# Softmax weights scaled on ScalarE ahead of the transposes, in place of a reciprocal that is spread, transposed and multiplied in after the values

## The chip, the cores and the metric

The kernel runs on one core of one Trainium2 chip. The metric is the device time of one execution in microseconds (us), lower is better; a kernel's time is the median of its runs. The engines of the core are named as the profile names them: PE (TensorE, with its weight loads as PEld), DVE (VectorE), ACT (ScalarE), POOL (GpSimd) and SP (SyncE, which only issues DMAs here). Each has its own in-order queue.

## What is computed

Attention over 4 batches and 8 heads with 576 rows of 64 numbers, in which every row keeps its 32 largest scores; then a feed-forward part over 2304 tokens; then a part with eight experts, of which each token uses at most one. Cut to the lines of the attention, which the change is in, and of the part that runs beside it:

```python
scores = scale * np.matmul(q, k.transpose(0, 1, 3, 2))
kth = np.partition(scores, -top_k, axis=-1)[..., -top_k:-top_k + 1]
mask = scores >= kth
scores = np.where(mask, scores, -1000000000.0)
scores = scores - np.max(scores, axis=-1, keepdims=True)
attn = np.exp(scores)
attn = attn / (np.sum(attn, axis=-1, keepdims=True) + 1e-09)
return np.matmul(attn, v).astype(np.float32)
...
h = x @ w_in
g = np.maximum(h, 0.0) + alpha * np.minimum(h, 0.0)
return (g @ w_out).astype(np.float32)
```

The division by the sum can be done before the product with v or after it; the change moves it from after to before.

## The kernel before

**Units.** The attention is cut into 80 units (class `Unit`). A full unit is 128 rows of q of two heads (one pair) of a batch; a mixed unit (`mix`, 16 of the 80) holds the last 64 rows of both heads as one 128-row block, so it has one "head" of 576 columns where a full unit has two. The 80 units lie in eight work items, two for each batch: blocks 0 and 1 of the rows for the four pairs (8 full units), then blocks 2, 3 and the mixed one (12 units).

**What one unit does, by its methods.** `scores` (PE) makes q times k in PSUM; `copy` (ACT) brings it to SBUF as `sb`; `fold` and `round` (DVE) find the 32nd largest of each row; `exp` (ACT) writes the exponentials to `Ex`; `weights` (DVE) zeroes what lies under the threshold and adds up each row's sum into `st`; `recip` (DVE) takes the reciprocals; `spread` (ACT) writes them as a block `rb` 128 columns wide; `turn` (PE) transposes `Ex` in eight or four pieces plus a last one, and behind that `rb` (L523) or, in a mixed unit, the reciprocals themselves (L526); `evac` (ACT) copies the transposes from PSUM to `PT`, and the transposed reciprocals to `R` (L538, L543); `values` (PE) multiplies with v into `px`; `out` multiplies `px` by `R` on DVE into `xf` (L560), ACT rounds that to `xh` (the tile `x`, L562), and POOL later subtracts the two for the low half (L111).

**What sets the order.** `main` walks over steps; in step kx it works on units kx-2 to kx+2 at once. A step has 14 slots. The table `STEP` says at which slot which method runs, and for which unit: `(5, -1, "turn", 0)` is slot 5 of the step, for the unit one behind. After each slot's methods `slot` puts in pieces of the feed-forward part from the queue `todo`, against a budget: six matmuls at a time, first of the up projection (`up`, L628, with a Relu on ACT, L638, the second half of the activation on DVE, L641, a rounding to `g` on ACT, L647, and a subtraction on POOL, L111), then of the down projection (`down`, L674, copied out by ACT, L683). The up projection writes to two PSUM banks (`pm`), and a bank is free again when L641 has read it. So each engine's order is fixed when the program is built, and at run time an engine waits only where what it needs isn't there yet. While the first work item's units run, `todo` also holds the conversion of the feed-forward weights (L281 to L304).

The routing (`rows`), and after the attention the experts, follow; neither is touched.

## Time and profile before

| | |
|---|---|
| median of 3 runs | 1017.21 us (1016.46 to 1017.65) |
| the profiled execution | 1015.15 us, of which the profile's span is 1013.4 us |
| busy in the span | PE 889.1 us (88%), DVE 825.0 (81%), ACT 624.8 (62%), POOL 347.1 (34%) |
| mean granted TensorE clock | 0.957 of full speed |

By time: up to some 150 us the weights are converted beside the first units; from there to some 820 us attention units and feed-forward run together; then the feed-forward of the last work item and the experts remain. Busy time is the time in which an engine had an instruction under way. Instructions overlap with the next one's start, so what an instruction takes of its engine is read from start to start, and is shorter than its own duration. The chain that ended last is followed back from the end of the program: at each step to what released it, or to the instruction before it on its engine.

### The profile page before, as it was taken

The page shows a single profiled execution, that of the slowest core. Times are in us where ns is not written, and L with a number is a line of the kernel's source. Part 1 is how long each engine was busy: PE and PEld are TensorE (multiplying, and loading weights), DVE is VectorE, ACT ScalarE, POOL GpSimd, SP SyncE. Part 2 cuts the span into 40 slices and gives each one's busy share as a digit, 9 for nine tenths or more (in the row PEclk, how much of TensorE's full clock was granted, in tenths as well). Part 3 has the DMA queues.
Part 4 walks back from the last instruction along what each step waited for, and adds up shares of the span by engine and source line. Part 5 has one row for each costly group of instructions (what it writes and reads, how often), then busy time and mean ns, then how long its engine had stood idle before and what let it go on. Part 6 is the DMA issues. An engine that isn't in the chain of part 4 may idle for free.

```text
span 1013.4 us, 21379 instructions
## 1 busy us (share of the span) xinstructions
PE 889.1 (88%) x7074; PEld 786.7 (78%) x7074; DVE 825.0 (81%) x2859; ACT 624.8 (62%) x1669; POOL 347.1 (34%) x544
## 2 busy tenths in 40 slices
PE   4335569899999989999998899999978999999995
PEld 2234458798999889989997899899978988987541
DVE  5999999999998899989997999899799632366410
ACT  7869767666775567667655766775566434365320
POOL 4866653322430243234212432431133134023100
PEclk9976679999999899999999999999999999999998
DMA  8978985666656476766655676765564769979994
GB/s 244 329 261 239 309 261 188 219 227 185 245 190 236 143 228 204 243 219 214 220 198 159 219 227 234 241 224 192 181 189 179 250 230 416 352 243 384 398 398 149
DMA packets 133321, 244.90 MB, mean 242 GB/s; under 512 B 58831, under 2 KB 91599, under 8 KB 116817
## 3 DMA queue, kind: packets, MB, share of 16 engines
q1 hardware_dynamic: 129824, 239.42, 69.7%
q0 software_dynamic: 2176, 3.73, 1.0%
q8 instruction: 58, 0.95, 0.4%
q14 instruction: 63, 0.51, 0.2%
q10 hardware_dynamic: 1200, 0.30, 0.1%
HBM read 215.00 MB, written 28.92 MB: 241 GB/s over the span
## 4 chain that ended last, share of the span: by engine, by line
PE 59%; DVE 25%; ACT 4%; DMA 2%; issue 2%; POOL 1%; SPq 0%; POOLq 0%; DVEq 0%; ACTq 0%
PE pm L674 20%; PE pm L628 10%; DVE v L461 6%; PE px L553 5%; PE pm L1018 5%; PE ps L1018 4%; DVE Ex L494 4%; PE ps L431 3%; PE pt L520 3%; DVE ra L641 3%; DVE F L464 3%; DVE F L452 3%; DVE m L452 2%; PE ps L425 1%; PE px L549 1%
## 5 line engine op out<-in xcount | busy, mean ns | idle before, releaser
L628 PE MATMUL pm<-x,wr 128*128 128x256 f32 (+1 forms) x1536 | 248.5, 309 | 24.4 <-DVE ra L641 18.5
L628 PEld LDWEIGHTS pm<-x,wr 128*128 128x128 f32 x1536 | 214.9, 193 | 36.4 <-DVE ra L641 23.8
L674 PE MATMUL pm<-g,wr 128*128 128x256 f32 (+1 forms) x1536 | 234.5, 302 | 1.8 <-DVE ra L641 1.2
L674 PEld LDWEIGHTS pm<-g,wr 128*128 128x128 f32 x1536 | 208.9, 189 | 7.0 <-issue 4.6
L461 DVE MAX8 v<-F 128x8 f32<-128x72 f32 (+2 forms) x576 | 213.1, 405 | 0.9
L111 POOL TENSOR_TENSOR g<-ra,g 128x256 fp32r<-128x256 f32 (+1 forms) x128 | 103.2, 815 | 198.7 <-DVE st L499 59.8
L464 DVE MATCH_REPLACE8 F<-v,F 128x72 f32<-128x72 f32 (+1 forms) x432 | 122.9, 290 | 0.0
L494 DVE SCALAR_TENSOR_TENSOR Ex<-sb,v,Ex 128x577 f32<-128x577 f32 x144 | 122.2, 876 | 0.0
L436 ACT ACTIVATE sb<-ps 128x288 f32<-128x288 f32 x224 | 80.0, 411 | 67.9 <-PE ps L431 53.8
L486 ACT ACTIVATE Ex<-sb,st 128x576 f32<-128x576 f32 x144 | 104.8, 775 | 0.1
L647 ACT ACTIVATE g<-ra 128x256 fp32r<-128x256 f32 (+1 forms) x128 | 57.3, 448 | 72.6 <-DVE ra L641 70.4
L532 ACT ACTIVATE PT<-pt 128x512 f32<-128x512 f32 x144 | 86.7, 603 | 22.4 <-PE pt L520 22.0
L111 POOL TENSOR_TENSOR x<-xf,x 128x128 fp32r<-128x128 f32 (+1 forms) x80 | 37.3, 467 | 176.4 <-DVE st L499 120.7
L641 DVE SCALAR_TENSOR_TENSOR ra<-ra,slope,pm 128x256 f32<-128x256 f32 (+1 forms) x128 | 64.7, 507 | 38.7 <-ACT ra L638 38.1
L553 PE MATMUL px<-PT,vt 128*64 128x128 f32 (+1 forms) x1280 | 90.2, 288 | 0.0
L520 PE MATMUL pt<-ident,Ex 128*128 128x128 f32 x576 | 85.1, 281 | 4.3 <-ACT sb L436 4.3
L431 PE MATMUL ps<-kT,qT 64*128 64x288 f32 x576 | 80.0, 349 | 7.0 <-ACT kT L341 2.5
L553 PEld LDWEIGHTS px<-PT,vt 128*64 128x64 f32 x1280 | 70.8, 149 | 9.8 <-issue 2.0
L431 PEld LDWEIGHTS ps<-kT,qT 64*128 64x128 f32 x576 | 61.8, 212 | 20.8 <-issue 9.4
L638 ACT ACTIVATE ra<-pm 128x256 f32<-128x256 f32 (+1 forms) x128 | 52.6, 411 | 38.8 <-PE pm L628 37.4
L520 PEld LDWEIGHTS pt<-ident,Ex 128*128 128x128 f32 x576 | 70.3, 146 | 6.4 <-ACT sb L436 5.9
L452 DVE TENSOR_TENSOR F<-m 128x144 f32<-128x144 f32 (+2 forms) x240 | 66.0, 327 | 0.0
(356 smaller groups left out, 1484.4 us busy)
## 6 DMA issues: line engine op xcount, KB each, us to landing
wr<-win SPq DMA_DIRECT2D x64, 1024.0 KB, 5.1
wr<-wout SPq DMA_DIRECT2D x64, 1024.0 KB, 5.0
wd<-in_moe_w_dram SPq DMA_DIRECT2D x40, 512.0 KB, 11.5
wraw<-in_moe_w_dram SPq DMA_DIRECT2D x32, 512.0 KB, 7.9
wr<-in_moe_w_in_dram SPq DMA_DIRECT2D x16, 512.0 KB, 5.5
vt<-in_v_dram SPq DMA_DIRECT2D x32, 256.0 KB, 2.8
win<-cv SPq DMA_DIRECT2D x16, 512.0 KB, 4.5
wr<-in_moe_w_out_dram SPq DMA_DIRECT2D x16, 512.0 KB, 5.0
```

Of the source, the lines that this page charges most:

```text
L111: i = nc.gpsimd.tensor_tensor(o, a, b, op=OP.subtract)
L431: nc.tensor.matmul(self.ps[h, j][:, 0:HALF], lhsT=hd["q"][gp, a, u * 128 - hd["c0"]:(u + 1) * 128 - hd["c0"]], rhs=hd["k"][gp, b_, c0:c0 + ...
L452: gate[0] = nc.vector.tensor_tensor(o[:, n_], a[:, n_, 0:w], a[:, n_, w:2 * w], op=op)
L461: nc.vector.max(v8[:, h, r, :], F[:, h, 0:w])
L464: nc.vector.match_replace(out=F[:, h, 0:w], in_to_replace=v8[:, h, r, :], in_values=F[:, h, 0:w], imm_value=NEG)
L486: nc.scalar.activation(self.Ex[:, h, :], self.sb[:, h, :], AF.Exp, bias=self.st[:, 0, h:h + 1], scale=0.125)
L494: nc.vector.scalar_tensor_tensor(self.Exp[:, cs], self.sbp[:, cs], v8[:, h, 3, 7:8], self.Exp[:, cs], op0=OP.is_ge, op1=OP.mult, accum_out ...
L520: nc.tensor.transpose(pt[:, c * 128:(c + 1) * 128], P[:, c0:c0 + 128], ident)
L553: nc.tensor.matmul(x[h * 64:(h + 1) * 64, 0:n], lhsT=hd["vt"][:, h, c, :], rhs=rhs, start=False, stop=(c == SF - 1))
L628: nc.tensor.matmul(hp[:, 0:n], lhsT=w[:, (f % 2) * 8 + a * 4 + d, :], rhs=x[:, d, c0:c1], start=(i == 0), stop=(i == 3 * KD - 1))
L641: nc.vector.scalar_tensor_tensor(ra, ra, slope[:, f:f + 1], hp[:, 0:n], op0=OP.mult, op1=OP.add)
L674: nc.tensor.matmul(op_[:, 0:n], lhsT=w[:, 2 * f + a, :], rhs=g[(hf + ch) * 8 + f, sg][:, gg, 0:n], start=(i == 0), stop=(i == ni - 1))
```

## The change

Units from number 8 on (`NORM = 8`; `early`) no longer carry their reciprocals past the product with v. `recip` runs for them at the end of their own step, right behind `weights`, in place of slot 2 of the next step. A new method `norm` at slot 4 of the next step multiplies `Ex` by the reciprocals in place on ACT, one instruction for each head (576 columns; a mixed unit has one). `spread`, the transposes of `rb` or `st`, the copies to `R` and the multiplication on DVE are left out for them. `out` then has ACT read `px` twice, once rounding to `x`, once into `xf`. The first 8 units keep the old way. For all units the table moves `turn` from slots 5, 6 and 8 to 7, 8 and 10, and `evac` from slots 7, 8 and 10 to 9, 10 and 12.

```diff
--- before.py
+++ after.py
@@ -22,15 +22,15 @@
 NSLOT = 14
 STEP = [(0, 0, "exp", 0), (0, 0, "exp", 1), (0, 1, "fold"),
         (1, -2, "values"), (1, 2, "scores"), (1, 0, "certify"),
-        (2, -1, "recip"), (2, 1, "round", 0), (2, 2, "copy", 0),
+        (2, -1, "recip", 0), (2, 1, "round", 0), (2, 2, "copy", 0),
         (3, 2, "copy", 1),
-        (3, 0, "heads", 0), (4, 1, "round", 1),
-        (5, -1, "spread"), (5, -1, "turn", 0), (5, 0, "heads", 1),
-        (6, 1, "round", 2), (6, -1, "turn", 1),
-        (7, -1, "evac", 0),
-        (8, -2, "out"), (8, -1, "evac", 1), (8, 1, "round", 3), (8, 1, "rest"), (8, -1, "turn", 2),
-        (10, 0, "weights", 0), (10, -1, "evac", 2),
-        (11, 0, "weights", 1)]
+        (3, 0, "heads", 0), (4, -1, "norm"), (4, 1, "round", 1),
+        (5, -1, "spread"), (5, 0, "heads", 1),
+        (6, 1, "round", 2), (7, -1, "turn", 0),
+        (8, -2, "out"), (8, -1, "turn", 1), (8, 1, "round", 3), (8, 1, "rest"),
+        (9, -1, "evac", 0), (10, -1, "evac", 1), (10, -1, "turn", 2),
+        (10, 0, "weights", 0), (11, 0, "weights", 1), (11, 0, "recip", 1), (12, -1, "evac", 2)]
+NORM = 8
 AHEAD = 4
 EC = 32
 PH = 6
@@ -408,6 +408,7 @@
             self.exact, self.vi, self.lastu, self.end = exact, vi, lastu, False
             self.mix = u == SF
             self.nh = 1 if self.mix else 2
+            self.early = exact or ai >= NORM
             self.n_ = slice(0, self.nh)
             self.pt = {}
 
@@ -494,13 +495,20 @@
                 nc.vector.scalar_tensor_tensor(self.Exp[:, cs], self.sbp[:, cs], v8[:, h, 3, 7:8], self.Exp[:, cs],
                                                op0=OP.is_ge, op1=OP.mult, accum_out=st[:, 1, h:h + 1])
 
-        def recip(self):
+        def recip(self, at):
             st = self.st
-            nc.vector.reciprocal(st[:, 2, self.n_], st[:, 1, self.n_])
+            if at == self.early:
+                nc.vector.reciprocal(st[:, 2, self.n_], st[:, 1, self.n_])
+
+        def norm(self):
+
+            if self.early:
+                for h in range(self.nh):
+                    nc.scalar.activation(self.Ex[:, h, :], self.Ex[:, h, :], AF.Copy, scale=self.st[:, 2, h:h + 1])
 
         def spread(self):
             st = self.st
-            if not self.mix:
+            if not self.mix and not self.early:
                 self.rb = att.tile([128, 2, 64], F32, name="rb", tag="rb", bufs=2)
                 nc.scalar.activation(self.rb, st[:, 2, :, None].to_broadcast([128, 2, 64]), AF.Copy)
 
@@ -520,10 +528,12 @@
                     nc.tensor.transpose(pt[:, c * 128:(c + 1) * 128], P[:, c0:c0 + 128], ident)
             elif not self.mix:
                 nc.tensor.transpose(pt[:, 0:128], P[:, SB:SB + 128], ident)
-                nc.tensor.transpose(pt[:, 128:256], self.rb.rearrange("p h c -> p (h c)"), ident)
+                if not self.early:
+                    nc.tensor.transpose(pt[:, 128:256], self.rb.rearrange("p h c -> p (h c)"), ident)
             else:
                 nc.tensor.transpose(pt[0:64, 0:128], Ex[:, 0, SB:S], ident)
-                nc.tensor.transpose(pt[:, 128:256], self.st[:, 2, 0:1].to_broadcast([128, 128]), ident)
+                if not self.early:
+                    nc.tensor.transpose(pt[:, 128:256], self.st[:, 2, 0:1].to_broadcast([128, 128]), ident)
 
         def evac(self, h):
             PT, pt = self.PT, self.pt.get(h)
@@ -531,16 +541,18 @@
                 if h < self.nh:
                     nc.scalar.activation(PT[:, 4 * h:4 * h + 4, :].rearrange("p a b -> p (a b)"), pt, AF.Copy)
                 return
-            R = att.tile([128, 128], F32, name="R", tag="R", bufs=1)
-            self.R = R
+            if not self.early:
+                self.R = R = att.tile([128, 128], F32, name="R", tag="R", bufs=1)
             if not self.mix:
                 nc.scalar.activation(PT[:, 8, :], pt[:, 0:128], AF.Copy)
-                nc.scalar.activation(R, pt[:, 128:256], AF.Copy)
+                if not self.early:
+                    nc.scalar.activation(R, pt[:, 128:256], AF.Copy)
             else:
                 for g in range(2):
                     gp = slice(g * 64, (g + 1) * 64)
                     nc.scalar.activation(PT[gp, 8, 0:64], pt[0:64, g * 64:(g + 1) * 64], AF.Copy)
-                    nc.scalar.activation(R[gp, 0:64], pt[gp, 128 + g * 64:128 + (g + 1) * 64], AF.Copy)
+                    if not self.early:
+                        nc.scalar.activation(R[gp, 0:64], pt[gp, 128 + g * 64:128 + (g + 1) * 64], AF.Copy)
 
         def values(self):
             hd, PT = self.hd, self.PT
@@ -557,9 +569,13 @@
             n = 64 if self.mix else 128
             cols = slice(self.col, self.col + n)
             xf = att.tile([128, 128], F32, name="xf", tag="xf", bufs=2)
-            nc.vector.tensor_tensor(xf[:, 0:n], self.x[:, 0:n], self.R[:, 0:n], op=OP.mult)
             xh, xl = self.getx()
-            nc.scalar.activation(xh[:, self.p, cols], xf[:, 0:n], AF.Copy)
+            if self.early:
+                nc.scalar.activation(xh[:, self.p, cols], self.x[:, 0:n], AF.Copy)
+                nc.scalar.activation(xf[:, 0:n], self.x[:, 0:n], AF.Copy)
+            else:
+                nc.vector.tensor_tensor(xf[:, 0:n], self.x[:, 0:n], self.R[:, 0:n], op=OP.mult)
+                nc.scalar.activation(xh[:, self.p, cols], xf[:, 0:n], AF.Copy)
 
             def low():
                 sub(xl[:, self.p, cols], xf[:, 0:n], xh[:, self.p, cols].bitcast(F32))
```

How the order changes. Names in the rows: `sb` scores in SBUF, `Ex` exponentials, `st` sums and reciprocals, `pt` and `ps` PSUM tiles, `kT`, `raw` transposed k and its copy for the low half, `pm` a bank of the feed-forward part. Lines of the changed file are up to 16 higher.

**ACT**, in one step of batch 2 in which the up projection runs, from the last copy of the scores on. Before:

```order
L436 ACTIVATE sb_138<-pt 128x288
L647 ACTIVATE g<-ra 128x320
L341 ACTIVATE kT<-ps 128x512
L342 ACTIVATE raw__6611<-ps 128x512
L505 ACTIVATE rb<-st 128x128
L638 ACTIVATE ra<-pm 128x320
L532 ACTIVATE PT<-pt 128x512
L562 ACTIVATE x<-xf 128x128
L532 ACTIVATE PT<-pt 128x512
```

and now:

```order
L437 ACTIVATE sb_138<-pt 128x288
L507 ACTIVATE Ex_144<-Ex_144,st 128x576 x2
L663 ACTIVATE g<-ra 128x320
L341 ACTIVATE kT<-ps 128x512
L342 ACTIVATE raw__6511<-ps 128x512
L654 ACTIVATE ra<-pm 128x320
L574 ACTIVATE x<-px 128x128
L575 ACTIVATE xf<-px 128x128
L470 ACTIVATE st<-v_6424 128x2
L663 ACTIVATE g<-ra 128x320
L542 ACTIVATE PT<-pt 128x512
```

The two scalings stand right behind the copies of the scores and ahead of the next Relu (L638, now L654); `rb` is gone, `out` is two copies from `px`, and the copies to `PT` come later.

**PE**, the same step, from the transposes of k to the product with v. Before:

```order
L356 MATMUL ps<-ident,nat 128x128 x4
L628 MATMUL pm<-x,wr 128x320 x6
L520 MATMUL pt<-ident,Ex_144 128x128 x8
L628 MATMUL pm<-x,wr 128x320 x6
L522 MATMUL ps<-ident,Ex_144 128x128
L523 MATMUL ps<-ident,rb 128x128
L628 MATMUL pm<-x,wr 128x320 x24
L549 MATMUL px<-PT,vbd_93 128x128
```

and now:

```order
L356 MATMUL ps<-ident,nat 128x128 x4
L644 MATMUL pm<-x,wr 128x320 x12
L528 MATMUL pt<-ident,Ex_144 128x128 x8
L644 MATMUL pm<-x,wr 128x320 x12
L530 MATMUL ps<-ident,Ex_144 128x128
L644 MATMUL pm<-x,wr 128x320 x12
L561 MATMUL px<-PT,vbd_93 128x128
```

Six more matmuls of the feed-forward part stand ahead of the transposes, and 12 in place of 24 between the last transpose and the product with v; the transpose of `rb` is gone.

**DVE**, the end of that step. Before:

```order
L464 MATCH_REPLACE F<-v_6525,F 128x288 x2
L560 TENSOR_TENSOR xf<-px,R 128x128
L461 MAX v_6525<-F 128x8 x2
L641 SCALAR_TENSOR_TENSOR ra<-ra,slope,pm 128x320
L494 SCALAR_TENSOR_TENSOR Ex_144,st<-sb_136,v_6525,Ex_144 128x577 x2
L641 SCALAR_TENSOR_TENSOR ra<-ra,slope,pm 128x320
```

and now:

```order
L465 MATCH_REPLACE F<-v_6424,F 128x288 x2
L462 MAX v_6424<-F 128x8 x2
L657 SCALAR_TENSOR_TENSOR ra<-ra,slope,pm 128x320
L495 SCALAR_TENSOR_TENSOR Ex_144,st<-sb_136,v_6424,Ex_144 128x577 x2
L501 RECIPROCAL st<-st 128x2
L657 SCALAR_TENSOR_TENSOR ra<-ra,slope,pm 128x320
```

The multiplication is gone, and the reciprocal stands right behind the instructions whose sums it reads. The queues of SP and POOL hold the same instructions in the same order as before.

## Rows read from the trace of the kernel before

**Rows 1.** Chain that ended last, share of the span by engine.

```profile
PE 59%; DVE 25%; ACT 4%; DMA 2%; issue 2%; POOL 1%; SPq 0%; POOLq 0%; DVEq 0%; ACTq 0%
```

**Rows 2.** Busy us by window: start:end length, PE, PEld, DVE, ACT, POOL, clock, DMA share.

```profile
375.00:400.00 25.00, 22.11 (x215) 20.60 (x214) 24.34 (x78) 18.72 (x57) 11.42 (x18) 1.00 0.60 197
450.00:475.00 25.00, 24.91 (x207) 23.67 (x205) 23.74 (x82) 19.67 (x58) 13.85 (x21) 1.00 0.61 205
500.00:525.00 25.00, 25.00 (x211) 23.82 (x209) 22.53 (x78) 14.92 (x43) 3.17 (x6) 1.00 0.60 200
200.00:800.00 600.00, 573.79 (x5073) 537.04 (x5072) 563.90 (x2136) 393.68 (x1153) 184.78 (x330) 0.99 0.63 209
```

**Rows 3.** Chain in order of time: removed operations on it (start us, us, what).

```profile
155.08 0.11 PE ps L523
...
813.48 0.11 PE ps L526
...
162.81 0.20 DVE xf L560
...
780.99 0.20 DVE xf L560
...
441.84 0.17 ACT R L538
```

**Rows 4.** ACT in order of time, a step with up projection and a later one.

```profile
461.66 0.31 ACT L505 ACTIVATE rb<-st 128x128 f32<-128x128 f32 x1
461.86 0.44 ACT L638 ACTIVATE ra<-pm 128x320 f32<-128x320 f32 x1
462.18 0.61 ACT L532 ACTIVATE PT<-pt 128x512 f32<-128x512 f32 x1
462.65 0.33 ACT L562 ACTIVATE x<-xf 128x128 fp32r<-128x128 f32 x1
462.85 0.62 ACT L532 ACTIVATE PT<-pt 128x512 f32<-128x512 f32 x1
...
466.57 1.43 ACT L486 ACTIVATE Ex<-sb,st 128x576 f32<-128x576 f32 x2
```

**Rows 5.** Chain in order of time: 24 matmuls of the up projection.

```profile
463.50 3.52 PE pm L628 x24
```

**Rows 6.** Chain in order of time: the reciprocal, and a small DVE operation behind its input.

```profile
737.54 0.19 DVE rt L792
...
777.60 0.08 DVE st L499
```

**Rows 7.** Chain in order of time: two of its four passages through ACT (of the first, the end).

```profile
361.38 0.18 ACT PT L537
...
361.60 0.49 PE px L549 x2
...
550.43 1.31 ACT sb L436 x4
...
552.28 0.19 ACT rb L505
```

**Rows 8.** Waits: engine, line, waited for; us in total, times, longest.

```profile
ACT ra L638 <- PE pm L628: 37.4, 48, 2.9
```

**Rows 9.** DVE in order of time, behind the Relu of 461.86 us.

```profile
461.18 0.28 DVE L560 TENSOR_TENSOR xf<-px,R 128x128 f32<-128x128 f32 x1
461.38 1.41 DVE L461 MAX8 v<-F 128x8 f32<-128x576 f32 x2
462.70 0.53 DVE L641 SCALAR_TENSOR_TENSOR ra<-ra,slope,pm 128x320 f32<-128x320 f32 x1
```

**Rows 10.** Groups by line and shape: count, busy us, mean ns, idle before, releaser.

```profile
L532 ACT ACTIVATE PT<-pt 128x512 f32<-128x512 f32 x144 | 86.7, 603 | 22.4 <-PE pt L520 22.0
L560 DVE TENSOR_TENSOR xf<-px,R 128x128 f32<-128x128 f32 x64 | 17.9, 280 | 16.7 <-PE px L553 16.7
L452 DVE TENSOR_TENSOR m<-sb 128x576 f32<-128x576 f32 x64 | 57.1, 893 | 1.2 <-ACT sb L436 1.2
```

## The prediction

> **What bounds the kernel now.** I read first the chain that ended last. By engine it is 59% PE and 25% DVE, and only 4% ACT [rows 1]: time that is taken off ACT is worth almost nothing by itself, time taken off PE or DVE is worth as much as the chain runs through it. Second, the busy time by window. From 200 to 800 us, where attention units and feed-forward run together, PE is busy for 573.8 of 600 us and DVE for 563.9, so both are nearly full at once; ACT has 393.7 [rows 2], which leaves it a third. The stretches differ. In 500 to 525 the down projection runs: PE is full, ACT idles for 10 of 25 us. In 375 to 400 and 450 to 475 the up projection runs, each group of which costs DVE one instruction and ACT two: DVE is at 24.3 and 23.7, PE at 22.1 and 24.9, and ACT at 18.7 and 19.7 of 25 [rows 2]. So the question is whether ACT can take the work over there without coming late. Third, the chain in order of time, for how often the operations that go away lie on it; fourth, the engines in order of time in one step with up projection, for what each takes from start to start and how much room a late ACT has.
>
> **What goes away.** It counts from unit 8 on, that is from about 150 us, for 56 full and 16 mixed units. *PE:* the transpose of the spread reciprocals takes 0.11 us. The chain has 41 of them, 33 at L523 and 8 at L526, from 155 to 813 us [rows 3]; with two that are longer, 4.9 us. The other 31 are hidden behind DVE. *DVE:* the multiplication of px lasts 280 ns [rows 10], but from its start to the next one's it is 0.20 us [rows 9]. It is on the chain 27 times from 162 to 781 us, mostly with 0.20 [rows 3], 5.3 us in all. With it DVE's wait for px goes, 16.7 us at the full units [rows 10]; where DVE waits for PE the chain runs through PE, so I count nothing for it. *ACT:* the spread takes 0.20 us from start to start [rows 4] and the copy to R 0.17 [rows 3]; R is on the chain in six pieces, 1.0 us. Sum of what goes: 4.9 + 5.3 + 1.0 = **11.2 us**.
>
> **What comes in on DVE.** The reciprocal moves behind the instructions whose sums it reads. At its old place it cost 0.08 us, since its input was long there; a small operation that needs its forerunner's result takes 0.19 us, with 0.02 of waiting ahead of it [rows 6]. The bounds are thus 0 and 0.13 more per unit, and I take 0.13, as the order now has that dependence. The chain passes the end of `weights` some 16 times after unit 8: **2.1 us** back. The Relu's second half behind it on DVE comes that much later.
>
> **What comes in on ACT.** The scaling is not in the trace. The nearest row is the exponential of the same 576 columns, in the same place in SBUF, also with one operand per partition: 1.43 us for the two of a full unit [rows 4], so half of that, 0.72, for the one of a mixed unit. The copies of 512 columns to PT, 603 ns each [rows 10] and about 0.47 from start to start [rows 4], bound it from below at 1.0 us a pair. I take 1.43. `out` gets a second copy of 128 columns, 0.20 us [rows 4]. Net per full unit: 1.43 + 0.20 - 0.20 - 0.17 = 1.26 us; per mixed unit 0.72 plus a copy and less two short ones, some 0.7. That is 56 x 1.26 + 16 x 0.7 = 82 us more of ACT, about an eighth on top of what it has from 150 to 820 us: 14.9 of 25 becomes some 18 with the down projection, 19.7 becomes 22.6 with the up projection.
>
> In the down projection I cost this at nothing: ten idle us of 25 cover it, and if they did not, it would be 1.26 us a step. In the up projection the two scalings stand ahead of the next Relu, and what waits for that is DVE's L641, then the bank `pm`, then PE. In the step shown the Relu began at 461.86 and lasted 0.44 [rows 4], and DVE asked for it at 462.70 [rows 9]: 0.40 us of room, against a delay of 1.43 - 0.20 = 1.23. Here DVE would lose 0.83. But in 48 of the 128 groups ACT itself was waiting for PE before the Relu, 37.4 us in all [rows 8], and there the delay fits in. What surely shows is where the chain already runs through ACT from the scores' copies to what follows them. It does so four times, at 357, 365, 448 and 550 us; the first ends in PE waiting for PT, the last in the spread [rows 7]. Each gets 1.23 us longer: **4.9 us**. For the other steps I add **1 us**, between 0 and the 19 us of the slower rival below; I stay near the low end because the chain has hardly any ACT elsewhere [rows 1].
>
> **What only moves.** The transposes and the copies to PT come two slots later for every unit, the first 8 too. PE's six extra matmuls ahead of the transposes are those that stood behind them, so PE's work is the same; it now waits there for ACT's scaling, not for DVE's weights. Between the last transpose and the product with v stand 12 matmuls in place of 24, at 0.147 us each (24 take 3.52 us on the chain [rows 5]) still 1.8 us for three ACT instructions. That cover is why I cost the move at nothing; if it is gone, PE waits for PT as it does once now, at 361 us [rows 7]. What is late next there are the scores and the copies behind them. The new copies from px wait for nothing more: ACT has by then waited for scores that PE makes after px. No DMA is moved past another, and SP's and POOL's queues keep their order; POOL's subtraction for x starts a step later than `out` as before.
>
> **A rule against it.** The pair of exponentials takes ACT 1.43 us, and a two-input operation of the same 576 columns on DVE lasts 893 ns on the mean [rows 4, 10], so for float32 this trace shows no slower ACT. The Trainium skill ("ScalarE: Activation LUTs", Rules for kernel authors) would have a multiplication on VectorE, not ScalarE, naming a gain for bf16. By it the scalings would go to DVE: as an estimate 128 of them at 0.89 us would be 114 us on an engine that has 36 idle us between 200 and 800, and the kernel slower by over 70. The rows decide for ACT here.
>
> **The sum.** -11.2 + 2.1 + 4.9 + 1 = -3.2 us, against the profiled execution's 1015.15: 1012.0. That execution lies 2.06 us below the median of 1017.21, so I add them: **1014.0 us**.
>
> **The rivals.**
> *ACT comes late in the up projection (slower).* The place is the Relu behind the scalings. For it: 19.7 of 25 us busy and 0.40 us of room [rows 2, 4, 9]. Against it: the waits of rows 8. About half of the 72 units lie beside the up projection, 36; in 80 of 128 groups ACT was not waiting for PE, so some 22 steps would each lose 0.83, 19 us (18.7). Then -11.2 + 2.1 + 18.7 = +9.6: 1027 us. It decides from 11 such steps on, where 9.1 us of gain are used up. The skill's rule quoted above points this way too.
> *The gain is only half real (no change).* PE and DVE are both nearly full, so where one loses 0.1 or 0.2 us the other is the next limit at once. For it: 573.8 and 563.9 of 600 [rows 2]. Half of 10.2 us is 5.1; -5.1 - 1.0 + 2.1 + 4.9 + 1 = +1.9: 1019 us.
> *ACT hides all of it (more faster).* If the passages through ACT do not grow, since the moved copies to PT leave the Relu an earlier place, -11.2 + 2.1 = -9.1: 1008 us. For it: ACT's idle third; against it: rows 7.
> That the change doesn't take effect is no case: the order shows the transposes and multiplications gone from 72 units.
>
> **How the numbers follow.** A measurement of this kernel tells about 0.2% (2 us) from no change. Forecast 0.30, ACT hides all 0.21, half real 0.21, ACT late 0.28. The first two are faster by over 0.2%, 0.51 less a little that the forecast's own spread gives away: 0.50. Same 0.21; slower 0.29. The range reaches from 3 us under the best case, for waits of DVE that also go, to the slower rival: 1005 to 1027.
>
> **What would show it.** Right: PE busy some 8 us less, DVE some 14 less, ACT some 75 to 85 more; the scaling at 0.7 to 0.8 us; the chain's ACT share near 5% and its waits in the down projection unchanged. Wrong to the slow side: more idle time of DVE before L641 with the Relu as releaser, of PE before L628 with L641, or of PE before L549 with PT as releaser, in 450 to 475 and its like. Wrong to the fast side: those idle times unchanged, and the up projection's steps shorter by 0.2 us or more. What would overturn the whole account is a change before 150 us, where only the slots moved.

## The result and the profile after

The changed kernel takes **1030.97 us** (median of 4 runs, 1030.22 to 1033.51) against 1016.84 for the kernel before: a ratio of 1.0143, 95% interval 1.0123 to 1.0163. The forecast of 1014.0 and its range up to 1027 are missed on the slow side. The profiled execution took 1033.51 us, so its trace shows some 2.5 us more than the median.

From the page of the changed kernel, busy time by engine:

```profile
PE 892.4 (87%) x7002; PEld 779.2 (76%) x7002; DVE 827.4 (80%) x2787; ACT 681.6 (66%) x1725; POOL 354.8 (34%) x544
```

ACT has 57 us more than before (624.8), where 75 to 85 were forecast. PE and DVE were to have 8 and 14 us less and have 3.3 and 2.4 more. What the added instructions last, by line and shape:

```profile
L507 ACT ACTIVATE Ex<-Ex,st 128x576 f32<-128x576 f32 x128 | 94.0, 790 | 0.8 <-DVE st L501 0.8
L574 ACT ACTIVATE x<-px 128x128 fp32r<-128x128 f32 x56 | 16.1, 287 | 0.2
L575 ACT ACTIVATE xf<-px 128x128 f32<-128x128 f32 x56 | 16.6, 296 | 0.0
L501 DVE RECIPROCAL st<-st 128x2 f32<-128x2 f32 x64 | 10.5, 165 | 1.9
```

The scaling (L507) lasts what was taken for it: 790 ns each, and 1.43 to 1.46 us a pair. From the start of a pair to the start of what follows it is 1.33 us, as it is for the pair of exponentials that the price was read from, so the price taken was 0.1 us too high and not too low. The waits of the changed kernel (us in total, times, longest):

```profile
DVE ra L657 <- ACT ra L654: 47.7, 42, 4.6
...
PE px L561 <- ACT PT L547: 44.9, 15, 8.2
...
PE pt L528 <- ACT Ex L507: 9.6, 15, 1.9
...
ACT ra L654 <- PE pm L644: 30.6, 33, 3.1
```

and the two of them that the kernel before has too (there L641 and L638 are the Relu's two halves, L549 the product with v):

```profile
DVE ra L641 <- ACT ra L638: 38.1, 31, 3.9
...
PE px L549 <- ACT PT L537: 35.7, 10, 7.7
```

DVE waits 9.6 us longer for the Relu, PE 9.2 us longer for PT, and 9.6 us that are new for the scaled exponentials; ACT itself waits less for PE than in [rows 8]. So three waits for ACT have grown at once, and the waits alone don't tell which of them costs the time.

Where in the program it is lost is read by unit: the start of the product with v (L561) of each of the 80 units, in one trace less in the other. Beside the down projection almost every long step is **shorter by 0.11 to 0.13 us**, a transpose of the reciprocals. The losses are in two kinds of steps. *Short steps* are those ahead of a mixed unit, where `main` halves the feed-forward budget (its factor 0.5): 8 of them beside the up projection (units 11, 14, 31, 34, 51, 54, 71 and 74; the step of unit 14 has the last Relu of the up projection there, and matmuls of the down projection already), 7 beside the down projection. *First steps* are 12, the first four of each work item of 8 full units (units 20 to 23, 40 to 43 and 60 to 63), beside the up projection. Two short steps of the kernel before, from one product with v to the next (columns as in [rows 2]):

```profile
355.46:361.60 6.14, 5.84 (x62) 5.18 (x61) 4.84 (x18) 5.05 (x19) 3.75 (x7) 0.96 0.74 236
381.57:387.29 5.72, 5.56 (x64) 5.20 (x62) 5.58 (x21) 5.28 (x20) 4.23 (x7) 1.00 0.47 145
```

and the same two of the changed kernel:

```profile
360.50:368.25 7.75, 5.92 (x61) 4.90 (x59) 5.14 (x19) 6.86 (x20) 3.52 (x5) 1.00 0.86 236
388.86:396.15 7.29, 6.02 (x63) 4.99 (x61) 6.49 (x23) 6.94 (x22) 4.30 (x7) 1.00 0.55 184
```

These are the steps of units 31 and 34. This is the reading that the prediction lacked. **ACT was busy for 5.05 of 6.14 and 5.28 of 5.72 us in these steps before the change**; of the 25 us windows of [rows 2], 375 to 400 mixes the second of them with long steps and shows 18.7 of 25, and 450 to 475 (19.7) has no short step in it. Now ACT has 1.81 and 1.66 us more there, and the steps are 1.61 and 1.57 us longer. The first of these two steps in the changed kernel, in order of time. ACT:

```profile
362.34 0.71 ACT L437 ACTIVATE sb<-ps 128x288 f32<-128x288 f32 x2 [0.66 <-PE ps L432]
...
363.82 1.46 ACT L507 ACTIVATE Ex<-Ex,st 128x576 f32<-128x576 f32 x2
...
365.68 0.42 ACT L654 ACTIVATE ra<-pm 128x256 f32<-128x256 f32 x1
...
367.92 0.28 ACT L547 ACTIVATE PT<-ps 128x128 f32<-128x128 f32 x1
```

PE:

```profile
364.67 1.32 PE L528 MATMUL pt<-ident,Ex 128*128 128x128 f32 x8 [0.72 <-ACT Ex L507]
...
368.25 0.49 PE L561 MATMUL px<-PT,vbd 128*128 128x128 f32 x2 [0.73 <-ACT PT L547]
```

and DVE:

```profile
366.13 0.48 DVE L657 SCALAR_TENSOR_TENSOR ra<-ra,slope,pm 128x256 f32<-128x256 f32 x1 [2.40 <-ACT ra L654]
```

ACT's queue starts when PE has the scores (0.66 us of waiting) and runs on, but for 0.23 us, from 362.34 to the copy to PT at 367.92, for which PE then waits. The scaling stands in the middle of it, so the Relu, the copies to PT and the product with v are all late by it.

### The profile page after: what moved, and what is told of

It is laid out like the page before. It is cut to its first block, busy times and chain, and to the rows that moved or that the text cites. A ratio compares the mean times of both kernels' runs of the same rounds, so it can differ in the third digit from the quotient of the medians.

```text
span 1031.6 us, 21185 instructions
## 1 busy us (share of the span) xinstructions
PE 892.4 (87%) x7002; PEld 779.2 (76%) x7002; DVE 827.4 (80%) x2787; ACT 681.6 (66%) x1725; POOL 354.8 (34%) x544
## 5 line engine op out<-in xcount | busy, mean ns | idle before, releaser
L644 PE MATMUL pm<-x,wr 128*128 128x256 f32 (+1 forms) x1536 | 248.4, 310 | 20.0 <-DVE ra L657 15.2
L111 POOL TENSOR_TENSOR g<-ra,g 128x256 fp32r<-128x256 f32 (+1 forms) x128 | 106.0, 837 | 191.6 <-DVE v L462 62.1
L495 DVE SCALAR_TENSOR_TENSOR Ex<-sb,v,Ex 128x577 f32<-128x577 f32 x144 | 126.8, 909 | 1.2 <-ACT Ex L487 1.2
L657 DVE SCALAR_TENSOR_TENSOR ra<-ra,slope,pm 128x256 f32<-128x256 f32 (+1 forms) x128 | 64.7, 507 | 50.9 <-ACT ra L654 47.7
L528 PE MATMUL pt<-ident,Ex 128*128 128x128 f32 x576 | 87.6, 282 | 12.9 <-ACT Ex L507 9.6
L542 ACT ACTIVATE PT<-pt 128x512 f32<-128x512 f32 x144 | 83.2, 615 | 18.9 <-PE pt L528 18.4
L507 ACT ACTIVATE Ex<-Ex,st 128x576 f32<-128x576 f32 x128 | 94.0, 790 | 0.8 <-DVE st L501 0.8
L561 PE MATMUL px<-PT,vbd 128*128 128x128 f32 (+1 forms) x160 | 35.1, 304 | 45.1 <-ACT PT L547 44.9
```

Of the source, the lines that this page charges most:

```text
L111: i = nc.gpsimd.tensor_tensor(o, a, b, op=OP.subtract)
L495: nc.vector.scalar_tensor_tensor(self.Exp[:, cs], self.sbp[:, cs], v8[:, h, 3, 7:8], self.Exp[:, cs], op0=OP.is_ge, op1=OP.mult, accum_out ...
L507: nc.scalar.activation(self.Ex[:, h, :], self.Ex[:, h, :], AF.Copy, scale=self.st[:, 2, h:h + 1])
L528: nc.tensor.transpose(pt[:, c * 128:(c + 1) * 128], P[:, c0:c0 + 128], ident)
L542: nc.scalar.activation(PT[:, 4 * h:4 * h + 4, :].rearrange("p a b -> p (a b)"), pt, AF.Copy)
L644: nc.tensor.matmul(hp[:, 0:n], lhsT=w[:, (f % 2) * 8 + a * 4 + d, :], rhs=x[:, d, c0:c1], start=(i == 0), stop=(i == 3 * KD - 1))
```

## The experiments

All were run against the kernel before on the same chip; its median there was 1017.1 to 1018.2 us. "Slots alone" is the first of them, and "loss" without more is against it.

**Which part costs.** The slots without the scaling:

```diff
-NORM = 8
+NORM = 1000
```

> The changed table of slots with no unit scaled ahead (all units keep the transposed reciprocals and the multiplication). Against before (1016.8). Theory A, ScalarE's scalings come in the way of its own Relu and of PE's transposes in the steps with up projection: the moved slots alone cost only what the first 8 units lost, 2.3 us, and little after it: 1017 to 1021. Theory B, the moved slots themselves cost the time, since 12 matmuls no longer cover the copies to PT: without the gains of the removed operations this is at least as slow as the change, 1029 to 1040.

Measured 1018.11 us, ratio 1.0007 (0.9994 to 1.0020). The moved slots cost nothing that can be told, as forecast, though PE's wait for PT is 47.1 us already here: the growth of that wait in the change comes from the slots, and is no loss. In the trace the first 6 units do get 4.1 us later, by 112 us, but 3.4 us of that are given back by unit 9.

The other way round, the change with the old slots:

```diff
-(6, 1, "round", 2), (7, -1, "turn", 0), ...
+(5, -1, "turn", 0), (6, 1, "round", 2), (6, -1, "turn", 1), (7, -1, "evac", 0), ...
```

> The change with the transposes and the copies to PT back at their old slots, the scaling still ahead of them. Theory A: the scaling stays, and the transposes now ask for it two slots earlier, so as slow as the change or slower: 1030 to 1045. Theory B: the slots were the cost, the removed operations are a gain: 1008 to 1017.

Measured 1035.59 us, 1.0172 (1.0151 to 1.0192). Theory B has fallen: the later slots help the change, by 3 to 5 us. PE's wait for the scaled exponentials is 22.0 us here against 9.6.

The gain without the scaling:

```diff
 def norm(self):
-    if self.early:
+    if self.exact:
...
-nc.scalar.activation(xh[:, self.p, cols], self.x[:, 0:n], AF.Copy)
+nc.scalar.activation(xh[:, self.p, cols], self.x[:, 0:n], AF.Copy, scale=1.0 if self.exact else 0.125)
```

> The change without its scalings from unit 8 on: the normalisation is left out there, and the two copies of the output multiply by the constant 0.125 in place of it. It has the whole gain of the change and the later reciprocal, and none of the added load but one copy. If the removed operations are worth what the forecast took (11.2 - 2.1 = 9.1 us against the slots alone, 1018.1): 1008 to 1010. If PE's transpose alone counts, 72 times 0.12: also about 1009 to 1010. If half of it is taken by the other engine: 1013 to 1015.

Measured 1013.06 us, 0.9957 (0.9939 to 0.9975): **5.1 us under the slots alone, not 9.1**. By unit the gain is 0.12 in the long steps beside the down projection (PE's transpose), 0.20 at units 33, 53 and 73 (the multiplication on DVE), and next to nothing in most of the first steps.

The load without the gain, once where PE waits for it and once where it doesn't:

```diff
-NORM = 8
+NORM = 1000
...
-    if self.early:
+    if not self.exact and self.ai >= 8:
...
-nc.scalar.activation(self.Ex[:, h, :], self.Ex[:, h, :], AF.Copy, scale=self.st[:, 2, h:h + 1])
+nc.scalar.activation(self.Ex[:, h, :], self.Ex[:, h, :], AF.Copy, scale=1.0)
```

> The changed slots with no unit scaled ahead, and two ScalarE instructions of the scaling's size at the scaling's slot that multiply the exponentials by 1.0 in place: ScalarE's load and PE's wait for it, but nothing of what the change removes. Theory A1, the load costs and the wait for the scaled exponentials adds nothing of its own: as the load beside it, 1033.4: 1032 to 1036. Theory A2, PE's wait for them (9.6 us in the trace of the change) comes on top: 1038 to 1045.

```diff
-(4, -1, "norm")
+(4, 0, "norm")
...
-NORM = 8
+NORM = 1000
...
-    if self.early:
+    if not self.exact and self.ai >= 9:
...
-nc.scalar.activation(self.Ex[:, h, :], self.Ex[:, h, :], AF.Copy, scale=self.st[:, 2, h:h + 1])
+nc.scalar.activation(self.sb[:, h, :], self.sb[:, h, :], AF.Copy, scale=1.0)
```

> The changed slots with no unit scaled ahead, but with two ScalarE instructions of the scaling's size at the scaling's slot, multiplying by 1.0 in place the masked scores' source sb of the next unit, for which PE never waits and VectorE only much later. It has ScalarE's load without PE's wait for the scaled exponentials. Theory A1, the load makes the Relu late for VectorE: the cost of the change without its gain, 1031 plus some 7: 1032 to 1042. Theory A2, PE's transposes wait for the scaling: within 3 us of the run with the slots alone, 1017 to 1024. Theory B: the same as the slots alone, 1029 to 1040.

Measured 1032.09 us, 1.0144 (1.0116 to 1.0172), with PE's wait, and 1033.35, 1.0145 (1.0121 to 1.0169), without. A1 holds: ACT's time alone costs 14 to 15 us, and it adds nothing that PE asks for the multiplied exponentials; its wait for them, 6.6 us in the trace of the first, isn't paid on top. The load isn't quite that of the change: a multiplication by a constant lasts 0.70 us and a pair of them takes 1.15 us from start to start, not 1.33. That is 14% less, so some of the distance to the change's 17.9 (below) may lie there.

**Where it costs.** The changes of the starts, in us at unit 79 against the slots alone, by kind of step (a short step counts together with the one behind it, beside the up projection):

| run | to unit 8 | short, up | short, down | first | others | sum |
|---|---|---|---|---|---|---|
| the change | 0.7 | 8.6 | 2.5 | 6.5 | -2.8 | 15.5 |
| gain without scaling | -0.2 | -0.8 | -0.7 | 4.8 | -3.8 | -0.7 |
| 8 units left out | 0.4 | 2.1 | 2.5 | 7.9 | -2.2 | 10.8 |
| scalings apart | 0.2 | 6.1 | 4.4 | 5.6 | -1.8 | 14.5 |
| ahead of the copies | -0.3 | 7.5 | 1.1 | 2.7 | -2.8 | 8.2 |
| one pair, 8 units | -0.3 | 5.7 | 0.0 | 2.2 | 1.7 | 9.3 |
| two pairs, 8 units | -0.7 | 16.7 | 0.0 | 1.3 | 2.2 | 19.4 |

These are single executions. The 4.8 in the second row are two steps at a lower granted clock (below), and without them the gain is 5.5, close to the 5.1 of the medians. Other rows have such steps too. That of unit 20 has a stretch of 6.8 us at half clock in the rows "scalings apart" and "one pair" and none with the slots alone: 2.1 and 2.2 us of their first steps.

The change without eight units:

```diff
-self.early = exact or ai >= NORM
+self.early = exact or ai >= NORM and ai not in (11, 14, 31, 34, 51, 54, 71, 74)
```

> The change, but eight units (those whose transposes fall into a step with half the feed-forward budget beside the up projection) keep the transposed reciprocals and the multiplication. In the traces these steps lose 1.30, 1.33, 1.62, 1.57, 2.25, 1.37, 0.95 and 0.05 us net against before, 10.4 together. Theory A: that comes back, 1031.0 - 10.4: 1020 to 1023. Theory B, and a theory that every step with up projection loses alike: 1028 to 1032.

Measured 1026.05 us, 1.0079 (1.0061 to 1.0096): 5 us come back, between the two expectations. The 10.4 were too many: for six of the eight the step behind, which gives some back, wasn't counted, and the slots alone had moved these steps a little. Against the slots alone and with the step behind they lose 8.6, of which 6.5 are gone in the table. The other kinds stay.

One pair of dummy multiplications in these eight steps alone, and two:

```diff
-NORM = 8
+NORM = 1000
...
-if self.early:
-    for h in range(self.nh):
+if self.ai in (11, 14, 31, 34, 51, 54, 71, 74) and not self.exact:
+    for h in (0, 1):
...
+    for h in (0, 1) * 2:
```

> The changed slots with no unit scaled ahead, and one pair of multiplications by 1.0 in place of the exponentials, 1.43 us, at the scaling's slot for eight units alone: those whose transposes fall into a step with half the budget beside the up projection. Theory E: such a step waits for ScalarE's queue and gets longer by the pair less what ScalarE had idle there; in the traces of the change that was 1.1 us a step, so 1018.1 + 8 x 1.1: 1025 to 1028. Theory D (it is the whole stretch in which ScalarE has too little time): 1019 to 1022.

> The same with two such pairs for each of the eight units. Theory E: the first pair has used up the room, so the second costs its whole 1.43 us: 8 x 1.43 = 11.4 us above the run with one pair, 1035 to 1040. Theory D: twice what one pair costs, under 1030.

Measured 1023.22 us, 1.0057 (1.0036 to 1.0078), and 1034.73, 1.0161 (1.0135 to 1.0186). The first pair costs less than expected, 5.1 us by the medians, the second 11.5, and 11.0 in the table. That is 1.4 us a step on the mean, but the agreement with 1.43 is chance: a pair of these multiplications takes 1.15 us, and the steps are unlike. In the step of unit 31 with one pair, ACT:

```profile
361.66 1.27 ACT L507 ACTIVATE Ex<-Ex 128x576 f32<-128x576 f32 x2
362.81 0.40 ACT L341 ACTIVATE qT<-ps 128x256 fp32r<-128x256 f32 x1
```

The second pair costs 1.13 us in the steps of units 31 and 34, whose clock is the same in both traces, and 1.15 at unit 51: **one for one with its 1.15**. At units 11, 14, 54 and 74 it costs 1.5 to 2.25 us. There too PE's wait for the multiplied exponentials is longer by 1.15 us, 1.47 to 2.92 in all, but the granted clock falls as well: it is at half for 3.4 us, from within that wait or up to 1.5 us behind it, which it is not with one pair. At unit 71 both pairs together cost nothing. The first pair costs its whole length at units 14, 31, 34 and 51 (1.14 to 1.33), 0.4 at units 11 and 54, and nothing at 71 and 74. So four of the eight steps had no room left for ACT, and there the price of what is added is its length. In the change the same eight steps lose 1.1 each on the mean; its pair is 0.18 longer and its other units are scaled too, and what else makes the difference isn't settled.

The two scalings apart, with room for a Relu between:

```diff
-(3, 0, "heads", 0), (4, -1, "norm"), (4, 1, "round", 1),
+(3, 0, "heads", 0), (4, -1, "norm", 0), (4, 1, "round", 1),
...
-(6, 1, "round", 2), (7, -1, "turn", 0),
+(6, 1, "round", 2), (6, -1, "norm", 1), (7, -1, "turn", 0),
...
-if self.early:
-    for h in range(self.nh):
+if self.early and h < self.nh:
```

> The change with the two scalings of a full unit apart: the first stays at slot 4, the second stands at slot 6, so that a Relu can come between them. ScalarE's work is the same. Theory A1, what costs is that the next Relu stands behind a pair of 1.43 us: the Relu is late by half, and half of the 15 us that the load cost come back: 1022 to 1027. Rival D, ScalarE has too little time in these steps in whatever order: 1029 to 1033.

Measured 1029.83 us, 1.0122 (1.0095 to 1.0148): no more than 1 or 2 us. In the first steps units 21, 41 and 61 lose 0.2, 0.4 and nothing where the change loses 0.8, 1.0 and 0.5, so there the Relu behind the pair was the cause; without unit 20, whose clock differs, the first steps lose 3.5 in place of 6.1. The short steps beside the up projection get 2.5 back, and those beside the down projection lose 1.9 more. That the Relu stands behind a pair is thus a minor part, and the rival's place in the prediction was not the main one.

The scaling ahead of the scores' copies:

```diff
-(1, -2, "values"), (1, 2, "scores"), (1, 0, "certify"),
+(1, -2, "values"), (1, 2, "scores"), (1, 0, "certify"), (1, -1, "norm"),
...
-(3, 0, "heads", 0), (4, -1, "norm"), (4, 1, "round", 1),
+(3, 0, "heads", 0), (4, 1, "round", 1),
```

> The change with the scaling of a unit three slots earlier, right behind the exponentials and ahead of the copies of the scores. Its sums are there by then, and ScalarE's work is the same. Theory E, in a step with half the budget PE waits for a queue of ScalarE instructions that starts with the scores' copies, and the scaling lengthens it by its 1.43 us one for one: ahead of the copies it falls into the 0.6 to 1.3 us in which ScalarE waits for the scores, so a third to two thirds of the loss come back: 1021 to 1027. Theory D, ScalarE has too little time in these steps in whatever order: 1029 to 1033.

Measured 1024.95 us, 1.0069 (1.0048 to 1.0090): **half of the loss is back with the same work in the same queue**, so theory D has fallen. The short step of unit 31 shown above, ACT:

```profile
360.14 1.43 ACT L507 ACTIVATE Ex<-Ex,st 128x576 f32<-128x576 f32 x2
361.47 0.69 ACT L437 ACTIVATE sb<-ps 128x288 f32<-128x288 f32 x2
...
363.47 0.42 ACT L654 ACTIVATE ra<-pm 128x256 f32<-128x256 f32 x1
```

and DVE:

```profile
363.93 0.48 DVE L657 SCALAR_TENSOR_TENSOR ra<-ra,slope,pm 128x256 f32<-128x256 f32 x1 [1.47 <-ACT ra L654]
```

ACT no longer waits for the scores; the scaling fills that time, the Relu comes 2.0 us behind the copies' start in place of 3.3, DVE waits 1.47 for it, not 2.40, and the step lasts 6.67 us, not 7.75. The first steps lose 2.7 in place of 6.5, the short ones beside the down projection 1.1 in place of 2.5. The eight short steps beside the up projection still lose 7.5 us together, but unlike ones: six of them 3.9 in place of 7.7, those of units 11 and 54 more than in the change. PE in the step of unit 11, in this run:

```profile
170.75 0.44 PE L356 MATMUL ps<-ident,nat 128*128 128x128 f32 x2 [2.42 <-ACT sb L437]
```

and in the change:

```profile
171.38 0.44 PE L356 MATMUL ps<-ident,nat 128*128 128x128 f32 x2 [1.09 <-ACT sb L437]
```

Here PE waits for the copies of the scores themselves, now 1.33 us longer, the whole length of a pair (2.28 in place of 0.95 at unit 54), and the granted clock is then at half for 3.4 us, which it isn't in the change. In these two steps there is no place for the pair ahead of the copies either.

**Two that didn't help.** More feed-forward budget in the short steps, in the change and, as a control, in the kernel before:

```diff
-... * (0.5 if ok(kx + 1) and steps[kx + 1][2] == SF else 1.0) ...
+... * (0.75 if ok(kx + 1) and steps[kx + 1][2] == SF else 1.0) ...
```

> The change with three quarters of the feed-forward budget, in place of half of it, in the steps ahead of a mixed unit. Theory E: PE gets work for the time in which it waits there for ScalarE, and what it waits for is no later; the 8.6 us lost in these steps come back in good part: 1023 to 1027. Rival F, the added groups bring ScalarE a Relu and a copy each and so lengthen its queue by as much: 1029 to 1036.

> The kernel before with the same three quarters of the budget in these steps, to tell what that does without the scaling: 1015 to 1020 if it is the scaling that leaves PE room there; if it gains as much as in the change, the budget is a gain of its own and says nothing of the scaling.

Measured 1036.34 us, 1.0191 (1.0163 to 1.0218), and the control 1024.71, 1.0060 (1.0040 to 1.0080). The budget is a loss of its own, of 6 us without any scaling and 5 with it, so the pair says nothing on the scaling. It does fit that a short step is short of ACT already: each group that it gains brings a Relu and a copy.

The scalings on GpSimd:

```diff
-STEP = [(0, 0, "exp", 0), ...
+STEP = [(0, -1, "norm"), (0, 0, "exp", 0), ...
...
-nc.scalar.activation(self.Ex[:, h, :], self.Ex[:, h, :], AF.Copy, scale=self.st[:, 2, h:h + 1])
+nc.gpsimd.tensor_scalar(self.Ex[:, h, :], self.Ex[:, h, :], self.st[:, 2, h:h + 1], None, op0=OP.mult)
```

> The change with the scalings on GpSimd, which is idle two thirds of the time, issued at the start of the step. Its subtraction of 128x320 lasts 887 ns, so one of 128x576 is estimated at 1.6 us and a pair at 3.2. Theory E, only ScalarE's queue is the obstacle: the scaled exponentials are there before the transposes ask at slot 7 in the long steps, and the time is 1012 to 1022. Rival G, GpSimd comes too late in the short steps, and its other subtractions behind it are late for PE: 1025 to 1050.

Measured 1043.72 us, 1.0257 (1.0232 to 1.0282): rival G. The groups of that kernel:

```profile
L507 POOL TENSOR_SCALAR Ex<-Ex,st 128x576 f32<-128x576 f32 x128 | 261.1, 2049 | 129.2 <-DVE st L501 88.2 <-PE pm L644 13.9 <-DVE rc L801 9.6
...
L453 DVE TENSOR_TENSOR m<-m 128x288 f32<-128x288 f32 x64 | 45.1, 704 | 0.0
```

and the second of them in the kernel before:

```profile
L452 DVE TENSOR_TENSOR m<-m 128x288 f32<-128x288 f32 x64 | 30.8, 481 | 0.0
```

A scaling takes 2049 ns there, more than the 1.6 us estimated, and DVE's own operations get slower beside it (481 to 704 ns). DVE's wait for the Relu is down to 28.5 us, so ACT was relieved; the time is lost elsewhere, 13.5 us of it in the eight short steps beside the up projection (the change: 8.6). How it divides between late exponentials and slower DVE operations wasn't tested.

**Versions that keep the gain.** The scaling only where a step has room, first at the slots of the change, for 39 units:

```diff
-NORM = 8
+NORM = (13, 15, 16, 18, 19, 23, 24, ..., 76, 77, 78, 79)
...
-self.early = exact or ai >= NORM
+self.early = exact or ai in NORM
```

> The change with the scaling ahead for 39 units alone, those whose own step lost nothing in the comparison of the traces (most stand beside the down projection); the other 41 keep the transposed reciprocals and the multiplication, all at the changed slots. Theory A, ScalarE has room in these steps: the slots alone gave 1018.1, and 39 steps get 0.12 us shorter each, 4.7 us: 1012 to 1015, faster than before. Rival C, what is gained there is lost again in the next step that waits for something else: 1017 to 1020.

then ahead of the scores' copies, for 53 (the table of slots as in the run above that had the scaling there):

```diff
-NORM = 8
+NORM = (11, 14, 17, 20, 21, 29, 30, 31, 34, 37, 40, 41, 42, 48, 51, 54, 57, 71, 74)
...
-self.early = exact or ai >= NORM
+self.early = exact or ai >= 8 and ai not in NORM
```

> The scaling right behind the exponentials, as in the run that had it ahead of the scores' copies, and only for the 53 units whose own step lost nothing in that run's trace; the other 19 keep the transposed reciprocals. Theory E, where ScalarE's queue has room the gain is 0.12 us a unit: 53 x 0.12 = 6.4 us under the slots alone (1018.1): 1011 to 1013. Rival C, the losses only move to the next units: 1014 to 1020.

Measured 1014.81 us, **0.9979** (0.9965 to 0.9994), and 1014.04, **0.9971** (0.9954 to 0.9989). Both beat both kernels, by 2 to 3 us over the kernel before. The first has the gain that was expected of it: 4.2 us by its trace, 3.3 by the medians. The second should have been another 1.7 us faster; the medians differ by 0.8, which the intervals don't tell from nothing. In its trace three steps are longer than with the slots alone. Those of units 20 and 50, by 2.0 and 1.3 us, have more time at half clock. That of unit 65 is longer by 1.2 at full clock: PE waits 1.18 us for the copies of the scores, which stand behind the scaling. It had lost the same 1.2 in the run that the units were chosen by, so it did not belong among the 53. Without these three steps the trace lies 5.8 us under the slots alone, near E's 6.4, and by the medians it is 4.1; that leans to E, and doesn't show it.

## Why the prediction was wrong

Three terms, each with a run of its own: what moves (forecast 0), what goes less the later reciprocal (-9.1), ACT's part (+5.9). Measured: +0.7, -5.1, and 1030.97 - 1013.06 = **+17.9** (18.9 by the ratios).

*What only moves: right.* 0.7 us, within the uncertainty. But the sign that was to overturn the account, a change before 150 us, did appear (4.1 us) and meant nothing, since it was given back: a passing delay in a stage that PE doesn't fill was a bad test.

*What goes: right in kind, 4 us too large.* Each removed operation on the chain was counted with its whole duration [rows 3]. The transposes gave theirs in the long steps beside the down projection; DVE's 0.20 us showed as such at units 33, 53 and 73, while 27 were counted. The rival "half real" took -5.1 - 1.0 + 2.1 = -4.0, which is nearer to the -5.1 measured.

*Scaling's price: near enough.* A pair was taken at 1.43 us, which is from the start of the first to the end of the second; from start to start it takes 1.33, as the exponentials do. That an idle ACT hides it in the down projection is right for the long steps, which got shorter, and wrong for its short ones (2.5 us lost).

*The four passages: right.* The passages of [rows 7], priced at 4.9 us, lie in the steps of units 31, 32, 41 and 51. These lose 1.4, 1.2, 1.0 and 1.8 us against the slots alone, 5.4 together.

***"For the other steps I add 1 us" is the step that failed***, with the reading behind it: that ACT has a fifth of its time free beside the up projection. With 17.9 us for ACT in all and 5.4 in the four passages, the other steps cost some 12, by the difference. The fifth was read from windows of 25 us. The program makes long and short steps. In the two short ones shown ACT was already busy for 82 and 92% of the time, and in the first of them PE already waited for ACT's last copy before the next product with v (0.19 us). Windows cut at the steps' own bounds would have shown it in the trace of before. The argument from the chain (hardly any ACT on it) couldn't: ACT was just short of being the bound, and work that is just off the chain shows no share of it. The busy share alone is no price, though: unit 51's step had ACT at 77% and loses 2.5 us, unit 11's had 92% and loses 0.4, with the steps behind them. By the runs with pairs and the one with the scaling ahead of the copies, what decides is whether the added work falls into a queue at whose end PE or DVE waits.

*The slower rival* had 18.7 us for ACT, and 17.9 were measured, but the size agrees by accident: it put 0.83 us on each of 22 steps whose Relu stands behind a pair. The runs show 1.1 us in eight short steps, and the Relu as the cause in three units of the first steps. The time is that of two rivals at once, ACT late and the gain half real (1017.2 - 4.0 + 18.7 = 1031.9), and no case on the list combined them.

*The rule* of the Trainium skill ("ScalarE: Activation LUTs", Rules for kernel authors), that a multiplication belongs on VectorE, wasn't put to the test: no run has the scalings there. The 893 ns by which the prediction priced them on DVE are of an instruction with two inputs, and the scaling has one, so that estimate stands untested too. The instruction on ScalarE wasn't dear, 790 ns; its queue was.

*Of the signs named*, one of the slow ones came true and tells something: DVE's idle time before the Relu's second half (38.1 us before, 37.3 with the slots alone, 47.7 in the change). PE's before the product with v grew too, but with the slots alone as much. PE's before L628 with L641 as releaser did not grow (18.5 before, 15.2 now). PE's 8 and DVE's 14 us less did not come, and ACT's busy time grew by 57 us, not 75 to 85.

Open remains how the loss of the first steps is shared between the Relu and the collision below. The part behind unit 79 is 2.8 us longer in the change than before (18.2 us in the spans of the profiled executions, 15.4 at unit 79). That is no loss of the scaling: it is 196.4 us in the trace of before, the shortest of all, 199.2 in the change, 198.6 with the slots alone, and between 197.0 and 199.5 in the other runs. What moves it is open.

## What to carry to other kernels

Before work goes to an engine that is idle for a third of the time, look at the *shortest* repeating step, with windows cut at the step's own bounds, and ask who waits at the end of that engine's queue: where its queue has no gap left, the new work costs its full length. Then look for the place where that engine waits for another and put the work there; the same two instructions three slots earlier cost half, but cost their full length again in the two steps where PE waited for what came behind them. And count an operation removed from one of two nearly full engines only in the steps where that engine, and not the other, is full.

## What the runs showed of the hardware

**DVE and POOL slow each other.** In the step of unit 22 of the change, DVE's second masked sum and POOL's subtraction run at the same time. DVE, in order of time:

```profile
276.88 0.82 DVE L495 SCALAR_TENSOR_TENSOR Ex<-sb,v,Ex 128x577 f32<-128x577 f32 x1
277.62 0.08 DVE L495 DVE_READ_ACCUMULATOR Ex<-sb,v,Ex 128x1 f32 x1
277.62 1.43 DVE L495 SCALAR_TENSOR_TENSOR Ex<-sb,v,Ex 128x577 f32<-128x577 f32 x1
```

and POOL:

```profile
276.95 1.48 POOL L111 TENSOR_TENSOR g<-ra,g 128x320 fp32r<-128x320 f32 x1
```

The same POOL instruction has a mean of 887 ns in the kernel before; with the slots alone it takes 0.88 in this step and runs beside a search of the maximum on DVE, which isn't slowed. In the change POOL is later, behind copies that ACT makes after the scaling, and meets the masked sum. Both take 0.6 us more, the Relu's second half on DVE comes later by that, and PE waits 0.71 us for it. The first of the two masked sums runs beside the same subtraction for 0.75 us and isn't slowed, as if the subtraction waited for it and the second sum then for the subtraction; that order is an inference. In the trace of before the 85 masked sums that have no POOL instruction beside them last 0.79 to 0.82 us, and some of those that have one up to 1.83. In the GpSimd run DVE is slowed as well, as shown above.

**The granted clock falls in one kernel and not in another at the same place.** The stretch after a work item's end, in the run without scaling:

```profile
248.00:252.00 4.00, 4.00 (x16) 4.00 (x16) 3.09 (x15) 0.80 (x2) 2.19 (x3) 0.50 1.01 298
```

and with the slots alone:

```profile
248.00:252.00 4.00, 4.00 (x29) 3.81 (x28) 3.76 (x13) 1.76 (x5) 1.52 (x3) 1.00 0.95 251
```

PE paused ahead of that in both, for nearly the same time. Without scaling:

```profile
246.02 0.58 PE L836 MATMUL pm<-oh,tri 128*128 128x16 f32 x2 [2.95 <-ACT x L574]
```

and with the slots alone:

```profile
247.28 0.37 PE L836 MATMUL pm<-oh,tri 128*128 128x16 f32 x2 [2.88 <-DVE rc L817]
```

After the pause the clock is at half for 6.8 us (0.50, 1.2 of 2.4 GHz) in the one and full in the other; what decides between the two isn't shown. The step lasts 16.25 and 13.97 us. The run without scaling has two such steps in its trace, 4.8 us together; its 12 executions lie between 1009.53 and 1017.44, the profiled one at 1016.78. A difference of a few us between two single traces of this kernel may thus be clock alone; medians of many runs, or the steps at full clock, are what can be compared.
